# A planned attention kernel: fewer semaphore waits, phi(K) sums in column strips, and an order planned with queue times

## The chip, the cores and the metric

The kernel runs on one core of a Trainium2 chip. The metric is the device time of one execution in microseconds (us); lower is better. The engines are named as the profile names them: PE (matmul; PEld is its weight load), DVE (vector), ACT (scalar), POOL (GpSimd) and SP (here the queue that issues DMAs).

## What is computed

Two attention blocks over the same input `x` (2048 x 512, bf16), 32 heads of 16, mixed by a gate:

```python
g = sigmoid((x * gate_w).sum(-1))
# A: softmax attention
p = softmax(q @ k.T * 16 ** -0.5);  a = (p @ v) @ A_wo
# B: linear attention, phi(t) = where(t > 0, t + 1, exp(t)) + 1e-6
kv = phi(k).T @ v;  z = phi(k).sum(over the sequence)
b = ((phi(q) @ kv) / (phi(q) @ z + 1e-6)) @ B_wo
out = g * a + (1 - g) * b
```

## The kernel before

**A planner writes the order.** While the program is built, a Python planner keeps a clock for each engine, a cost for each step, and for each tile the time of its last write and reads. It emits again and again the step that can start first; a list of tasks with release and due times (the table `TS`, in rounds) and some settings (`DEF`) decide between steps. The five instruction streams that come out are fixed: each engine runs its own in order, and semaphores hold an instruction until what it needs is there. So a step that waits holds everything behind it on its engine.

**Block A** goes in 32 rounds (8 heads of one parity group, 512 queries). PE makes score tiles of 128 keys x 512 queries, up to four heads beside each other in the rows of the array (`ps<-Qz,KT`). A tile is exponentiated in one of two ways. ACT does two tiles with one Exp (line 722) into P. Or DVE makes 16-bit integers that, read as bf16, are a rough exponential (line 634 for two tiles, line 673 for one), and POOL adds two constants to them (line 699), so that three terms with weighted copies of V (Vs, line 931) make up the sum. So a tile of DVE's needs three PV matmuls, one of ACT's needs one. PV matmuls (`ps<-P,Vp`, `ps<-Z,Vp`, `ps<-Z,Vs`) stand four beside each other in the columns of the array, in one bank (bank 7) for a whole round. At a round's end DVE transposes that bank (L959); each second round it takes reciprocals (L969), multiplies (L971) and transposes into OAT (L974).

**Everything else is tasks** that share the remaining bank 4: projections K (L871), Q (L900) and V (L922); the gate (L936 to L952); phi(K) and phi(Q) (Exp into eb on ACT, L981; two passes on DVE, L982 and L983); M = x.T phi(K) (L1003); the sums of phi(K), `t_z` (L1015); KV (L1036); the denominators `t_den` (L1061 to L1065); block B's output `t_bout` (L1077), which a transposing DMA on SP puts into OBT, the former xnat; and at last 16 output blocks `t_final`, each with four matmul steps of the B part (`ps<-wB,xnat`), four of the A part (`ps<-wB,OAT`), a pass by gg (L1110 on ACT, L1112 on DVE) and a DMA.

**Q loads.** Each Q projection is written to QT (L900) and copied to Qz by eight DMAs on SP. **The gate** is written to DRAM by four DMAs and read back in another layout by one (`ge<-gdram`), then used by DVE (L949).

**Waits.** `deps_of` lists what an instruction depends on; `_Eng.add` turns that into semaphore waits and leaves out one that the same engine has already waited for. Where an instruction has more than one wait, the first in the list goes inside it, and the others become instructions of their own ahead of it, which only wait (EVENT_SEMAPHORE, shown at line 1331).

**Costs.** A step of column-strip matmuls (`pe4`) is planned as the columns at 2.4 per ns + 8 ns for each group of four, at least 110 ns; a DMA issued by the planner as 60 ns of SP. PV steps of less than four matmuls are held back up to `PWN` ns (900). Where the plan leaves PE idle, filler matmuls (`ps<-warm`) stand.

Of the kernel before, what the change touches and what calls it, by code (L numbers as in the profile page):

```python
# [34 lines left out]
class _Eng:  # L35
    def __init__(self, name, sem, pipe):
        self.name = name
        self.sem = sem
        self.pipe = pipe
        self.free = 0.0  # L40
        self.ops = []
        self.n = 0
        self.inc_idx = []
        self.inc_val = []
        self.semval = 0
        self.waited = {}
# [81 lines left out]
def bass_gated_mix__mha_block__linear_attn_block__prompt_kernel(  # L128
# [42 lines left out]
    with ExitStack() as es:  # L171
        _cnt = [0]

        def SB(shape, dt, name):
            _cnt[0] += 1
            return es.enter_context(nc.sbuf_tensor(f"{name}_{_cnt[0]}", list(shape), dt))
# [85 lines left out]
        r_outt = [R(f"outt{i}") for i in range(2)]  # L262
        r_ge, r_gg, r_gd = R("ge"), R("gg"), R("gd")

        def deps_of(E, reads, writes):
            deps = []
            for res in reads:
                if res.w is not None:
                    deps.append(res.w)
            for res in writes:  # L270
                if res.w is not None:
                    deps.append(res.w)
                deps.extend(res.r.values())
            if E is PE:
                deps = [d for d in deps if not (isinstance(d, _Ev) and d.E is PE)]
            return deps
# [598 lines left out]
        def t_q(n, fixed=None):  # L875
# [51 lines left out]
        def t_vs(t8, vb):  # L927
            yield ("WAIT", lambda: ("v", t8 // 2, 2 * vb) in flags and ("v", t8 // 2, 2 * vb + 1) in flags and (t8 < 2 or st["pv_round"] > t8_rounds[t8 - 2][-1]))
            sl = slice(32 * vb, 32 * vb + 32)
            for w in range(1, NTERM):  # L930
                yield dl(265, lambda w=w: nc.vector.tensor_scalar(Vs[:, t8 % 2, w - 1, sl, :], Vp[:, t8, sl, :], WTS[w], None, op0=ALU.mult),
                         [r_Vp[t8][2 * vb], r_Vp[t8][2 * vb + 1]], [r_Vs[t8 % 2][w - 1][vb]])
            yield ("FLAG", lambda: V_ready.add(("s", t8, vb)))

        def t_gate():
# [12 lines left out]
            yield ("DMA", ge[:], gdram.rearrange("(k p) -> p k", p=128), semGE, 16, 3000.0, [r_gd], [r_ge], "nc", True)  # L948
            yield dv(100, lambda: nc.vector.tensor_scalar(ge[:], ge[:], 1e30, None, op0=ALU.min), [r_ge], [r_ge])  # L949
            phi_free[0] = True  # L950
            yield dv(100, lambda: nc.vector.tensor_scalar(gg[:], ge[:], 1.0, None, op0=ALU.add), [r_ge], [r_gg])
# [3 lines left out]
        def aout(r):  # L955
# [9 lines left out]
            if par == 0:  # L965
# [8 lines left out]
            yield dl(636, lambda: nc.vector.transpose(OAT[:, t8, 512 * qc:512 * (qc + 1)], T2[:]), [r_T2], [r_OAT[t8][qc]])  # L974
# [2 lines left out]
        def phi(b, dst_ap, dst_res):  # L977
            yield ("WAIT", lambda: phi_free[0] or phi_free[1])
            i = 0 if phi_free[0] else 1
            phi_free[i] = False  # L980
            yield ac(476, lambda: nc.scalar.activation(eb[:, i, :], bank(b), ACT.Exp), [r_bank[b]], [r_eb[i]])  # L981
            yield dv(345, lambda: nc.vector.tensor_scalar(eb[:, i, :], eb[:, i, :], 1.0, 1e-6, op0=ALU.min, op1=ALU.add), [r_eb[i]], [r_eb[i]])  # L982
            yield dv(609, lambda: nc.vector.scalar_tensor_tensor(dst_ap, bank(b), 1.0 + 1e-6, eb[:, i, :], op0=ALU.add, op1=ALU.max),  # L983
                     [r_bank[b], r_eb[i]], dst_res)
            yield ("FREE", b)
            phi_free[i] = True
# [20 lines left out]
        def t_z():  # L1007
            yield ("WAIT", lambda: all(("phik", tb) in flags for tb in range(NKB)))
            b = yield ("BANK",)
            for i in range(NCC):  # L1010
                for h in range(2):
                    yield pe_step(8, 140, [mm(bank(b)[:, i:i + 1], phiK[:, tb, 128 * i:128 * (i + 1)], ones[:, 0:1], start=(tb == 0), stop=(tb == NKB - 1))
                                           for tb in range(8 * h, 8 * h + 8)], [*r_phiK[8 * h:8 * h + 8], r_ones], [r_bank[b]])
            for i in range(NCC):
                yield dv(200, lambda i=i: nc.vector.tensor_scalar(Zbd[:, i, :], zmask[:], bank(b)[:, i:i + 1], None, op0=ALU.mult),  # L1015
                         [r_bank[b], r_zmask], [r_Zb])
            yield ("FREE", b)
            yield ("FLAG", lambda: flags.add("z"))
# [32 lines left out]
        def t_den(qc):  # L1051
# [4 lines left out]
            for qbl in range(4):  # L1056
                for i in range(NCC):
# [216 lines left out]
        while True:  # L1274
# [113 lines left out]
```

## Time and profile before

| | |
|---|---|
| time, median of 3 runs | 684.74 us (684.66 to 685.08) |
| the profiled execution | 684.91 us, span 683.2 us |
| granted PE clock over the span, mean | 0.99 |
| instructions in the profile | 20908 |
| exponentials on ACT (L722) | 671 |
| passes on DVE for two tiles (L634), for one (L673) | 310, 86 |
| filler matmuls | 95 |

A row of the profile has the busy time of a group of instructions, the mean of one, and the idle time of its engine just before them with what ended it. "L722" is line 722 of the kernel. Matmuls overlap each other, and so do consecutive passes on ACT, DVE and POOL, so the mean duration of one is longer than the step from one start to the next. The clock column of a stretch is the share of full speed that PE was granted.

### The profile page before, as it was taken

To read this page: it belongs to the slowest core of one execution; us is meant where nothing else is said; L and a number is where in the kernel's file an instruction comes from. 1 tells how busy PE (TensorE), PEld (TensorE's weight loads), DVE (VectorE), ACT (ScalarE), POOL (GpSimd) and SP (SyncE) were. 2 spreads that over 40 slices of the span, in tenths; PEclk is the share of its full clock that TensorE was granted. 3 is DMA by queue.
4 is the path that set the end of the run, shared out by engine and by line. 5 is a ranking of instruction groups with operands and counts; after the bars stand their busy time and mean duration, and the time that the engine had idled before them with its cause. 6 is when DMAs were issued, how large, how long until landed. Compare 5 with 4: busy or idle time off the path is not lost.

```text
span 683.2 us, 20908 instructions
## 1 busy us (share of the span) xinstructions
PE 645.9 (95%) x8412; PEld 192.7 (28%) x8412; DVE 576.0 (84%) x691; ACT 645.7 (95%) x712; POOL 436.5 (64%) x736
## 2 busy tenths in 40 slices
PE   8999899999999999999999999999999999999995
PEld 3422222222323222223322223222222222222222
DVE  5788689898876777889999899889889888989892
ACT  6799799999999999999999999999999999999991
POOL 4465577566755567676655566667666677878781
PEclk9999999999999999999999999999999999999998
DMA  5700000001010000200000101101000200000000
GB/s 130 222 24 23 4 2 4 8 8 26 2 40 2 2 1 2 51 8 2 2 4 15 25 9 34 10 25 25 25 10 17 33 17 18 1 10 10 10 10 32
DMA packets 35208, 15.39 MB, mean 23 GB/s; under 512 B 26532, under 2 KB 35108, under 8 KB 35112
## 3 DMA queue, kind: packets, MB, share of 16 engines
q1 hardware_dynamic: 34056, 13.79, 8.5%
q8 instruction: 67, 1.10, 0.7%
q10 hardware_dynamic: 1056, 0.26, 0.2%
q14 instruction: 29, 0.24, 0.1%
HBM read 6.30 MB, written 2.11 MB: 12 GB/s over the span
## 4 chain that ended last, share of the span: by engine, by line
PE 60%; ACT 14%; DVE 11%; issue 9%; POOL 3%; DMA 2%; SPq 0%; POOLq 0%; ACTq 0%; DVEq 0%
PE ps L327 60%; ACT P L722 13%; DVE Z L634 6%; POOL Z L699 3%; DVE T L959 1%; DVE Z L673 1%; DVE OBn L1077 1%; DMA xnat<-OBn 1%; DMA xnat<-in_A_x_dram 1%; DMA ge<-gdram 0%; ACT eb L981 0%; DVE T L971 0%; SPq L311 0%; DVE Vp L922 0%; DVE outt L1112 0%
## 5 line engine op out<-in xcount | busy, mean ns | idle before, releaser
L722 ACT ACTIVATE P<-ps 128x1024 bf16<-128x1024 f32 x671 | 629.1, 1054 | 16.7 <-PE ps L327 15.0
L699 POOL INT64_ADD Z<-Z x718 | 431.4, 616 | 228.5 <-DVE Z L634 203.9
L634 DVE TENSOR_SCALAR Z<-ps 128x1024 int16<-128x1024 f32 x310 | 377.3, 1217 | 72.4 <-PE ps L327 59.3
L327 PE MATMUL ps<-Qz,KT 32*128 32x512 bf16 x2048 | 262.5, 385 | 18.7 <-DVE Z L634 8.3
L327 PE MATMUL ps<-P,Vp 128*17 128x512 bf16 x1342 | 232.8, 385 | 1.3 <-DVE T L959 0.6
L327 PE MATMUL ps<-Z,Vs 128*17 128x512 bf16 x1412 | 228.2, 383 | 1.1 <-DVE Z L634 0.7
L327 PE MATMUL ps<-Z,Vp 128*17 128x512 bf16 x706 | 160.2, 384 | 0.4 <-DVE T L959 0.4
L327 PEld LDWEIGHTS ps<-Qz,KT 32*128 32x128 bf16 x2048 | 68.9, 91 | 269.1 <-ACT P L722 233.9
L327 PEld LDWEIGHTS ps<-P,Vp 128*17 128x17 bf16 x1342 | 51.3, 88 | 67.7 <-issue 40.2
L327 PEld LDWEIGHTS ps<-Z,Vs 128*17 128x17 bf16 x1412 | 51.6, 88 | 54.0 <-issue 35.0
L673 DVE TENSOR_SCALAR Z<-ps 128x512 int16<-128x512 f32 x86 | 58.1, 676 | 0.3 <-PE ps L327 0.3
L327 PE MATMUL ps<-xT,wA 128*32 128x512 bf16 (+1 forms) x528 | 37.5, 382 | 4.1 <-DVE phiK L983 3.2
L327 PEld LDWEIGHTS ps<-Z,Vp 128*17 128x17 bf16 x706 | 35.3, 88 | 12.8 <-issue 6.8
L327 PE MATMUL ps<-warm 128*17 128x512 bf16 (+8 forms) x104 | 30.9, 356 | 1.4 <-POOL warm L381 1.4
L959 DVE STREAM_TRANSPOSE T<-ps 128x512 f32<-128x512 f32 x32 | 22.7, 709 | 7.4 <-PE ps L327 7.4
L327 PE MATMUL ps<-wB,OAT 128*32 128x512 bf16 x256 | 21.2, 393 | 2.7 <-DVE OAT L974 2.7
L983 DVE SCALAR_TENSOR_TENSOR phiK<-ps,eb 128x512 bf16<-128x512 f32 x32 | 21.9, 685 | 0.8
L327 PE MATMUL ps<-wA,xT 128*32 128x256 bf16 x512 | 20.8, 275 | 0.4 <-DVE Vp L922 0.3
L327 PE MATMUL ps<-phiK,xnat 128*32 128x512 bf16 x256 | 19.5, 382 | 0.4 <-DVE Zbd L1015 0.4
L981 ACT ACTIVATE eb<-ps 128x512 f32<-128x512 f32 x32 | 19.9, 620 | 0.0
L327 PE MATMUL ps<-xT,wB 128*32 128x512 bf16 x256 | 19.6, 383 | 0.2 <-DVE phiK L983 0.2
L327 PE MATMUL ps<-wB,xT 128*32 128x512 bf16 x256 | 19.3, 383 | 0.3 <-DVE phiK L983 0.2
(73 smaller groups left out, 238.0 us busy)
## 6 DMA issues: line engine op xcount, KB each, us to landing
out_dram<-outt SPq DMA_DIRECT2D x16, 128.0 KB, 1.7
Qz<-QT SPq DMA_DIRECT2D x120, 16.0 KB, 1.8
wB<-in_B_wqkv_dram SPq DMA_DIRECT2D x3, 512.0 KB, 6.6
xnat<-in_A_x_dram SPq DMA_DIRECT2D x3, 512.0 KB, 8.6
wA<-in_A_wqkv_dram SPq DMA_DIRECT2D x10, 128.0 KB, 3.0
xnat<-in_A_x_dram SPq DMA_DIRECT2D x4, 128.0 KB, 3.3
wB<-in_B_wo_dram SPq DMA_DIRECT2D x1, 512.0 KB, 4.3
wB<-in_A_wo_dram SPq DMA_DIRECT2D x1, 512.0 KB, 3.8
```

The lines of the kernel that those rows point to most:

```text
L327: return lambda: nc.tensor.matmul(o, lhsT=l, rhs=r, start=start, stop=stop, skip_group_check=True)
L634: res.append(C(DV, 400, 1135, lambda: nc.vector.tensor_scalar(Z[:, zs[0], :], bank(5, 2), ZB, 0.0, op0=ALU.add, op1=ALU.max), [r_bank[5], ...
L673: res.append(C(DV, prio, 606, lambda b=b, z=z, h=h: nc.vector.tensor_scalar(Z[:, z, 512 * h:512 * (h + 1)], bank(b), ZB, 0.0, op0=ALU.add, ...
L699: return C(PO, 300, 160 + 0.416 * (hi - lo), lambda: nc.gpsimd.int64_add(Z[:, zw, lo:hi].bitcast(I64), Z[:, z0, lo:hi].bitcast(I64), cst), ...
L722: return C(AC, 500, 434 * n + 42, lambda: nc.scalar.activation(P[:, slot, 0:512 * n], bank(2 * g, n), ACT.Exp, scale=ESC), [r_bank[2 * g + ...
L959: yield dv(637, lambda: nc.vector.transpose(T1[:, par, :], bank(7)), [r_bank[7]], [r_T1[par]])
L981: yield ac(476, lambda: nc.scalar.activation(eb[:, i, :], bank(b), ACT.Exp), [r_bank[b]], [r_eb[i]])
L983: yield dv(609, lambda: nc.vector.scalar_tensor_tensor(dst_ap, bank(b), 1.0 + 1e-6, eb[:, i, :], op0=ALU.add, op1=ALU.max), [r_bank[b], r_ ...
L1077: yield dv(609, lambda: nc.vector.tensor_tensor(OBn[:, o, :].rearrange("p (h d) -> p h d", d=16), bank(b).rearrange("p (h d) -> p h d", d= ...
```

## The change

Four things are changed together.

1. **Waits.** Each engine keeps with every semaphore increment a copy of what it had waited for by then (`snap`). Who waits for that increment takes over all that the copy holds, and later waits for those are left out. `deps_of` sorts the dependencies by the planned time, the latest first, so the latest goes inside the instruction.
2. **Sums of phi(K).** `ones` has 64 columns, not 2. Before, each of the 64 products used a full 128 x 128 phi(K) block against one column of ones; now each is four matmuls, one for 32 columns of the array, against 64 columns of ones. The result is read from column 64 i of the bank.
3. **Planned costs.** SP is charged 630 ns for a Qz load or the strided gate load, 1290 ns for a transposing DMA and 380 ns for others. `pe4` is charged 4 ns a group over its columns, at least 57 ns. Where DVE and POOL use the port that they share at the same time, the later is delayed (`_Port`, `port`). Some durations and DMA times are other numbers.
4. **The order.** Settings (`DEF`) and due times (`TS`) are others, and with the new costs the whole order comes out anew. In `TS`, `t_bout` for query chunk qc is released at round 15.9 + 6.2 qc, before at 16.2 + 1.11 qc, and due at 16.9 + 4.2 qc, before at 17.9 + 2.5 qc; so its last four steps (34.5) are released after the last of the 32 rounds' scores.

```diff
+            if isinstance(d, _Ev):
+                for k2, v2 in d.E.snap[val - 1].items():
+                    if self.waited.get(k2, 0) < v2:
+                        self.waited[k2] = v2
...
+            self.snap.append(dict(self.waited))
...
-    DEF = {"SKEW": 4, "DSL": 0.0, "DTOL": 500.0, "PWE": 0.0, "PWT": 0.0, "PWN": 900.0, "TPR": 650, "RIDE": 1200.0, "HP": 115.0, "HD": 115.0, "NDB": 2, "SLK": 50.0, "UEX": 0.2, "TOP": 800, "B4": 1, "ROOM": 4, "STP": 2}
+    DEF = {"SKEW": 4, "DSL": 80.0, "DTOL": 500.0, "PWE": 0.0, "PWT": 0.0, "PWN": 400.0, "TPR": 620, "RIDE": 1200.0, "HP": 115.0, "HD": 115.0, "NDB": 2, "SLK": 50.0, "UEX": 0.2, "TOP": 420, "B4": 1, "ROOM": 3, "STP": 2}
...
-        ones = SB([128, 2], BF16, "ones")
+        ones = SB([128, 64], BF16, "ones")
...
+                deps.extend((res.tr[e2], d) for e2, d in res.r.items())
+            deps.sort(key=lambda v: -v[0])
...
+            if E is DV and isinstance(dur, _Port):
+                if port["p0"] <= start < port["p1"]:
+                    dur = max(dur, port["p1"] - start + dur.tail)
+                port["d0"], port["d1"] = start, start + dur + E.pipe
+            elif E is PO:
+                if port["d0"] <= start < port["d1"]:
+                    dur = max(dur, port["d1"] + 470.0 - E.pipe - start)
+                port["p0"], port["p1"] = start, start + dur + E.pipe
...
-            return ("OP", PE, len(groups) * max(cols / 2.4 + 8, 110.0), fns, reads, writes, "col")
+            return ("OP", PE, len(groups) * max(cols / 2.4 + 4, 57.0), fns, reads, writes, "col")
...
-                    yield pe_step(8, 140, [mm(bank(b)[:, i:i + 1], phiK[:, tb, 128 * i:128 * (i + 1)], ones[:, 0:1], start=(tb == 0), stop=(tb == NKB - 1))
-                                           for tb in range(8 * h, 8 * h + 8)], [*r_phiK[8 * h:8 * h + 8], r_ones], [r_bank[b]])
+                    yield pe4(64, [mm4(bank(b)[:, 64 * i:64 * (i + 1)], phiK[:, tb, 128 * i:128 * (i + 1)], ones[:], tb == 0, tb == NKB - 1)
+                                   for tb in range(8 * h, 8 * h + 8)], [*r_phiK[8 * h:8 * h + 8], r_ones], [r_bank[b]])
...
+                iss = 1290.0 if tr is True else 630.0 if tr == "nc" or c.name[0] == "Q" else 380.0
```

Three places of the new order. The first is DVE where it comes to the gate (`ge`). The rows from QT on, before:

```order
L900 TENSOR_SCALAR QT<-ps 128x512
L971 TENSOR_TENSOR T_25<-T_23,rec 128x2x16x16
L634 TENSOR_SCALAR Z<-ps 128x1024
L974 STREAM_TRANSPOSE OAT<-T_25 128x512
L982 TENSOR_SCALAR eb<-eb 128x512
L634 TENSOR_SCALAR Z<-ps 128x1024
L949 TENSOR_SCALAR ge<-ge 128x16
L983 SCALAR_TENSOR_TENSOR phiK<-ps,eb 128x512
```

and in the changed kernel (its line numbers are 22 higher here):

```order
L922 TENSOR_SCALAR QT<-ps 128x512
L656 TENSOR_SCALAR Z<-ps 128x1024
L996 STREAM_TRANSPOSE OAT<-T_25 128x512
L695 TENSOR_SCALAR Z<-ps 128x512
L656 TENSOR_SCALAR Z<-ps 128x1024
L953 TENSOR_SCALAR Vs<-Vp 128x576
L656 TENSOR_SCALAR Z<-ps 128x1024
L1004 TENSOR_SCALAR eb<-eb 128x512
L971 TENSOR_SCALAR ge<-ge 128x16
L1005 SCALAR_TENSOR_TENSOR phiK<-ps,eb 128x512
```

`ge` moved back: five steps stood between QT and it, now seven. The second place is SP from the gate's way out to DRAM on, before (`waits` shows which semaphores; `s_gd` counts the gate's arrival in DRAM):

```order
L311 DMA gdram<-eb 1x512 [waits s_act]
L311 DMA gdram<-eb 1x512 x3
L311 DMA Qz<-QT 16x512 [waits s_dve]
L311 DMA Qz<-QT 16x512 x3
L311 DMA Qz<-QT 16x512 [waits s_pe]
L311 DMA Qz<-QT 16x512 x2
L310 DMA ge<-gdram 128x16x1 [waits s_gd]
L311 DMA Qz<-QT 16x512
```

and in the changed kernel:

```order
L333 DMA gdram<-eb 1x512 [waits s_act]
L333 DMA gdram<-eb 1x512 x3
L333 DMA Qz<-QT 16x512 [waits s_dve]
L333 DMA Qz<-QT 16x512 x2
L332 DMA ge<-gdram 128x16x1 [waits s_gd]
L333 DMA Qz<-QT 16x512 x5
```

The load of `ge` went ahead of four Qz loads, and the wait of the second half of the Qz loads for PE is left out. The third place is the end of PE's stream, from the last PV matmuls ahead of the output blocks on, before:

```order
L327 MATMUL ps<-wB,xnat 32x512 x16
L327 MATMUL ps<-wB,OAT 32x512 x12
L327 MATMUL ps<-P,Vp 17x512
L327 MATMUL ps<-Z,Vs 17x512 x4
L327 MATMUL ps<-P,Vp 17x512
L327 MATMUL ps<-Z,Vs 17x512
L327 MATMUL ps<-Z,Vp 17x512
L327 MATMUL ps<-P,Vp 17x512
L327 MATMUL ps<-Z,Vs 17x512 x2
L327 MATMUL ps<-P,Vp 17x512 x2
L327 MATMUL ps<-Z,Vs 17x512 x4
L327 MATMUL ps<-wB,OAT 32x512 x16
```

(the first two rows stand there four times in turn, these being the last), and in the changed kernel:

```order
L349 MATMUL ps<-KVbd,phiK 32x128 x16
L349 MATMUL ps<-Z,Vs 17x512 x4
L349 MATMUL ps<-warm 17x512
L349 MATMUL ps<-warm 17x192
L349 MATMUL ps<-Z,Vs 17x512 x2
L349 MATMUL ps<-KVbd,phiK 32x128 x16
L349 MATMUL ps<-wB,xnat 32x512 x16
L349 MATMUL ps<-wB,OAT 32x512 x12
L349 MATMUL ps<-wB,xnat 32x512 x16
L349 MATMUL ps<-wB,OAT 32x512 x20
```

The last PV matmuls went ahead of the four output blocks, and the last four steps of `t_bout` (`KVbd,phiK`), which were done long before, stand among them now.

More of the change, by code (lines that the diff above doesn't have):

```diff
@@ L46, in __init__ @@
         self.waited = {}
+        self.snap = []
         self.cands = []
@@ L85, in add, with __new__ @@
             self.inc_val.append(self.semval)
+            self.snap.append(dict(self.waited))
         self.ops.append((waits, fn, inc, dma_sem))
         return _Ev(self, idx)
+class _Port(float):
+    def __new__(cls, dur, tail):
+        p = float.__new__(cls, dur)
+        p.tail = tail
+        return p
 class _Res:
@@ L263, in bass_gated_mix__mha_block__linear_attn_block__prompt_kernel @@
         r_ge, r_gg, r_gd = R("ge"), R("gg"), R("gd")
+        port = {"p0": 0.0, "p1": 0.0, "d0": 0.0, "d1": 0.0}
         def deps_of(E, reads, writes):
@@ L268, in deps_of @@
                 if res.w is not None:
-                    deps.append(res.w)
+                    deps.append((res.tw, res.w))
             for res in writes:
                 if res.w is not None:
[L272 to L276, printed above, removed]
+                    deps.append((res.tw, res.w))
+                deps.extend((res.tr[e2], d) for e2, d in res.r.items())
+            deps.sort(key=lambda v: -v[0])
+            return [d for _, d in deps if not (E is PE and isinstance(d, _Ev) and d.E is PE)]
         def emit(E, dur, fns, reads=(), writes=(), name=""):
@@ L906, in t_q @@
                     p0 = 32 * j + 16 * par
-                    yield ("DMA", Qz[p0:p0 + 16, s, par, :], QT[p0:p0 + 16, a, :], semQ[s], tot, 2500.0, [r_QT[a]], [r_Qz[s][par]], False, j == 0)
+                    yield ("DMA", Qz[p0:p0 + 16, s, par, :], QT[p0:p0 + 16, a, :], semQ[s], tot, 2200.0, [r_QT[a]], [r_Qz[s][par]], False, j == 0)
             for par in range(2):
@@ L930, in t_vs @@
             for w in range(1, NTERM):
-                yield dl(265, lambda w=w: nc.vector.tensor_scalar(Vs[:, t8 % 2, w - 1, sl, :], Vp[:, t8, sl, :], WTS[w], None, op0=ALU.mult),
+                yield dl(_Port(216, 84), lambda w=w: nc.vector.tensor_scalar(Vs[:, t8 % 2, w - 1, sl, :], Vp[:, t8, sl, :], WTS[w], None, op0=ALU.mult),
                          [r_Vp[t8][2 * vb], r_Vp[t8][2 * vb + 1]], [r_Vs[t8 % 2][w - 1][vb]])
@@ L947, in t_gate @@
             r_gd.w = _Raw(semGD, 64)
-            yield ("DMA", ge[:], gdram.rearrange("(k p) -> p k", p=128), semGE, 16, 3000.0, [r_gd], [r_ge], "nc", True)
+            yield ("DMA", ge[:], gdram.rearrange("(k p) -> p k", p=128), semGE, 16, 3600.0, [r_gd], [r_ge], "nc", True)
             yield dv(100, lambda: nc.vector.tensor_scalar(ge[:], ge[:], 1e30, None, op0=ALU.min), [r_ge], [r_ge])
@@ L970, in aout @@
             t2 = T2[:].rearrange("p (q a d) -> p a q d", a=2, d=16)
-            yield dl(642, lambda: nc.vector.tensor_tensor(t2, t1[:, :, :, 0:16], rec[:].unsqueeze(3).to_broadcast([128, 2, 16, 16]), ALU.mult),
+            yield dl(_Port(593, 465), lambda: nc.vector.tensor_tensor(t2, t1[:, :, :, 0:16], rec[:].unsqueeze(3).to_broadcast([128, 2, 16, 16]), ALU.mult),
                      [*r_T1, r_rec], [r_T2])
@@ L981, in phi @@
             yield ac(476, lambda: nc.scalar.activation(eb[:, i, :], bank(b), ACT.Exp), [r_bank[b]], [r_eb[i]])
-            yield dv(345, lambda: nc.vector.tensor_scalar(eb[:, i, :], eb[:, i, :], 1.0, 1e-6, op0=ALU.min, op1=ALU.add), [r_eb[i]], [r_eb[i]])
+            yield dv(_Port(337, 199), lambda: nc.vector.tensor_scalar(eb[:, i, :], eb[:, i, :], 1.0, 1e-6, op0=ALU.min, op1=ALU.add), [r_eb[i]], [r_eb[i]])
             yield dv(609, lambda: nc.vector.scalar_tensor_tensor(dst_ap, bank(b), 1.0 + 1e-6, eb[:, i, :], op0=ALU.add, op1=ALU.max),
@@ L1011, in t_z @@
                 for h in range(2):
[L1012 to L1013 removed]
+                    yield pe4(64, [mm4(bank(b)[:, 64 * i:64 * (i + 1)], phiK[:, tb, 128 * i:128 * (i + 1)], ones[:], tb == 0, tb == NKB - 1)
+                                   for tb in range(8 * h, 8 * h + 8)], [*r_phiK[8 * h:8 * h + 8], r_ones], [r_bank[b]])
             for i in range(NCC):
[L1015 removed]
+                yield dv(200, lambda i=i: nc.vector.tensor_scalar(Zbd[:, i, :], zmask[:], bank(b)[:, 64 * i:64 * i + 1], None, op0=ALU.mult),
                          [r_bank[b], r_zmask], [r_Zb])
@@ L1064, in t_den @@
             dv_ap = dn[:, a, :].rearrange("p (q h) -> p q h", q=4)
-            yield dl(215, lambda: nc.vector.tensor_tensor(dv_ap, dv_ap, ge[:, 4 * qc:4 * qc + 4].unsqueeze(2).to_broadcast([128, 4, 32]), ALU.mult),
+            yield dl(_Port(196, 68), lambda: nc.vector.tensor_tensor(dv_ap, dv_ap, ge[:, 4 * qc:4 * qc + 4].unsqueeze(2).to_broadcast([128, 4, 32]), ALU.mult),
                      [r_dn[a], r_ge], [r_dn[a]])
@@ L1315, in bass_gated_mix__mha_block__linear_attn_block__prompt_kernel @@
                 _, o, i, sem, tot, lat, rd, wr, tr, chk = c.fns[1]
-                fin = dma(SP, o, i, sem, tot, lat, reads=rd, writes=c.writes, transpose=(tr is True), noncontig=(tr == "nc"), name=c.name)
+                iss = 1290.0 if tr is True else 630.0 if tr == "nc" or c.name[0] == "Q" else 380.0
+                fin = dma(SP, o, i, sem, tot, lat, reads=rd, writes=c.writes, transpose=(tr is True), noncontig=(tr == "nc"), name=c.name, issue=iss)
                 if not chk:
```

2 lines of the change are left out of this document (1 added, 1 removed).

## The prediction

> **What bounds the kernel now.** I read the page first: shares, chain, groups.
>
> ```profile
> PE 645.9 (95%) x8412; PEld 192.7 (28%) x8412; DVE 576.0 (84%) x691; ACT 645.7 (95%) x712; POOL 436.5 (64%) x736
> ...
> PE 60%; ACT 14%; DVE 11%; issue 9%; POOL 3%; DMA 2%; SPq 0%; POOLq 0%; ACTq 0%; DVEq 0%
> ...
> L722 ACT ACTIVATE P<-ps 128x1024 bf16<-128x1024 f32 x671 | 629.1, 1054 | 16.7 <-PE ps L327 15.0
> ...
> L634 DVE TENSOR_SCALAR Z<-ps 128x1024 int16<-128x1024 f32 x310 | 377.3, 1217 | 72.4 <-PE ps L327 59.3
> ...
> L673 DVE TENSOR_SCALAR Z<-ps 128x512 int16<-128x512 f32 x86 | 58.1, 676 | 0.3 <-PE ps L327 0.3
> ```
>
> PE and ACT are both at 95%. ACT has one job that nobody shares, 671 exponentials of two score tiles each. By stages, columns being length, then busy time of PE, PEld, DVE, ACT, POOL, then clock and DMA:
>
> ```profile
> 400.00:540.00 140.00, 131.88 (x1795) 40.27 (x1797) 125.70 (x146) 137.42 (x153) 93.45 (x156) 1.00 0.11 22
> 540.00:666.80 126.80, 122.57 (x1470) 32.95 (x1473) 111.44 (x124) 125.73 (x135) 96.63 (x164) 1.00 0.04 11
> 666.80:683.20 16.40, 8.48 (x137) 3.59 (x129) 3.97 (x6) 1.44 (x3) 1.13 (x2) 0.80 0.10 33
> ```
>
> Up to 666.8 ACT has hardly a gap, and PE is 94 to 97% covered. After that stands a tail of 16.4 us in which everything is idle by turns. The price of an exponential is its start-to-start time, since consecutive ones overlap (timeline of ACT):
>
> ```profile
> 118.96 0.62 ACT L981 ACTIVATE eb<-ps 128x512 f32<-128x512 f32 x1
> 119.44 3.81 ACT L722 ACTIVATE P<-ps 128x1024 bf16<-128x1024 f32 x4
> 123.08 0.66 ACT L981 ACTIVATE eb<-ps 128x512 f32<-128x512 f32 x1
> ```
>
> Four take 123.08 - 119.44 = 3.64 us, 0.91 each. So time can go in three ways: fewer exponentials, the few places where ACT stands, and the tail. The sum is made against the profiled execution, 684.9 us (span 683.2), 0.2 above the median 684.74.
>
> **The waits that are left out.** Instructions that only wait:
>
> ```profile
> L1331 ACTq EVENT_SEMAPHORE  x580: 17/17/38, 8.0 to 679.8; - x194
> L1331 PEldq EVENT_SEMAPHORE  x410: 51/51/374, 3.2 to 671.2; - x137
> L1331 POOLq EVENT_SEMAPHORE  x394: 17/17/43, 26.2 to 666.6; - x197
> L1331 DVEq EVENT_SEMAPHORE  x317: 21/21/50, 6.2 to 679.3; - x159
> ```
>
> The changed program keeps 3 of ACT's, 18 of DVE's, none of POOL's, and 407 of PE's. ACT's 577 x 17 ns would be 9.8 us if they stood in the stream. But 580 waits stand ahead of 712 instructions, and the run of four above still went at 0.91; they pass while the instruction before is at work. ACT: nothing taken. On PE the number stays; what changes is which wait is inside, and a stand-alone one that comes last delays its matmul by up to 51 ns.
>
> ```profile
> PE ps L327 <- DVE Z L634: 9.1, 32, 0.8
> ...
> PEld ps L327 <- DVE Z L634: 5.1, 17, 0.4
> ```
>
> 49 x 51 ns = 2.5 us at most, 0 at least: I take **-1.0**.
>
> **The gate's load.** SP, DVE, PE and ACT around 70 us, then the waits of 66 to 76 us, then a stretch with its clock:
>
> ```profile
> 63.91 4.32 SPq L311 DMA_DIRECT2D Qz<-QT  x7
> 68.27 0.59 SPq L310 DMA_DIRECT2D ge<-gdram  x1
> ```
> ```profile
> 71.54 0.17 DVE L949 TENSOR_SCALAR ge<-ge 128x16 f32<-128x16 f32 x1 [2.79 <-DMA ge<-gdram]
> ...
> 72.36 0.93 PE L327 MATMUL ps<-xT,wA 128*32 128x512 bf16 x8 [2.74 <-DVE phiK L983]
> ...
> 73.88 1.02 ACT L722 ACTIVATE P<-ps 128x1024 bf16<-128x1024 f32 x1 [3.41 <-PE ps L327]
> ```
> ```profile
> ACT P L722 <- PE ps L327: 3.9, 2, 3.4
> ```
> ```profile
> 72.00:76.00 4.00, 3.64 (x30) 0.59 (x30) 2.97 (x7) 1.61 (x2) 1.28 (x2) 0.57 0.00 0
> ```
>
> The planner charged 60 ns for a DMA issue; seven Qz issues took 4.32 us, 0.62 each, and `ge` stood behind them. DVE came to `ge` 2.79 us early, all DVE work queued behind it, PE stopped, ACT lost 3.9 us. In the new order three Qz issues stand between QT and `ge`, not seven: 1.9 us of queue, then 71.54 - 68.27 = 3.3 to landing, 5.2 after QT. DVE has after QT three full passes, a half, a transpose, a Vs and an eb pass ahead of `ge`:
>
> ```profile
> L982 DVE TENSOR_SCALAR eb<-eb 128x512 f32<-128x512 f32 x32 | 14.6, 455 | 3.3 <-ACT eb L981 3.3
> ...
> L974 DVE STREAM_TRANSPOSE OAT<-T 128x512 bf16<-128x512 bf16 x16 | 11.2, 700 | 0.1
> ```
>
> 3 x 1.217 + 0.676 + 0.700 + 0.455 = 5.5 us even without Vs and without a wait (each pass overlaps the next by under 0.1), so `ge` is there when DVE is. What is late next is nothing on this path: the phi pass behind `ge` has its operands. I take **-3.9**; ends 0 and -3.9.
>
> **The sums of phi(K).** PE, two windows, and ACT's waits of 205 to 224 us:
>
> ```profile
> 211.17 0.55 PE L327 MATMUL ps<-ones,phiK 128*128 128x1 bf16 x16
> ```
> ```profile
> 209.00:212.40 3.40, 3.11 (x52) 1.36 (x44) 2.81 (x4) 3.40 (x4) 2.16 (x4) 1.00 0.00 0
> 212.40:215.90 3.50, 3.44 (x30) 0.70 (x30) 1.50 (x3) 2.47 (x4) 1.88 (x4) 0.51 0.02 5
> ```
> ```profile
> ACT P L722 <- PE ps L327: 1.3, 2, 0.9
> ```
>
> After a stretch of one-column matmuls the clock was 0.51 for 3.5 us, and ACT lost 1.3. With 64 columns in four strips the array works longer, so I expect no drop: -1.3, ends 0 and -1.7 (half of 3.4). Against it stand 256 matmuls for 64. The nearest row is the block product, 16 matmuls in 0.41:
>
> ```profile
> 538.11 0.41 PE L327 MATMUL ps<-KVbd,phiK 128*32 128x128 bf16 x16 [0.64 <-DVE OBn L1077]
> ```
>
> A step of 32 lasts at most 0.8, against about 0.3 for 8 one-column ones (0.55 for 16): 8 steps, 0 to +4 us of PE; I take +1.2, half hidden. Together **-0.7**.
>
> The Trainium skill (TensorE: Matmul & The Clock Gate, What's actually happening) has the clock drop after an idle window of about 3.4 us. Of the two drops here the first is near to that (PE idle 2.74), the second is not (PE covered 3.11 of the 3.40 before it); by the rule alone the strips would change nothing there, and this term would be +0.6, the sum 677.3.
>
> **The new order.** Counted over the whole program: exponentials 671 to 667, half passes on DVE (line 673) 86 to 94, groups of PV matmuls 899 to 927 since a partial group now goes after 400 ns, not 900. Fewer exponentials: 4 x 0.91 = **-3.6** (ends -3.6 and 0, if PE sets the pace). The 8 halves cost DVE 8 x 0.676 = 5.4 us, covered by its idle 107; if that cover were gone, 5.4. A PV group is 0.22 (start to start):
>
> ```profile
> 672.20 0.38 PE L327 MATMUL ps<-Z,Vs 128*17 128x512 bf16 x1
> ...
> 672.42 0.38 PE L327 MATMUL ps<-Z,Vp 128*17 128x512 bf16 x1
> ```
>
> 28 x 0.22 = 6.2 us on an engine that is 95% covered; part replaces filler matmuls (95 to 87). Ends 0 and +6.2; near the PE rows' 94 to 97% I take a third, **+2.0**. Early on, the new order holds 6,400 filler columns ahead of the last K tile of the first group, not 3,968, at 0.22 us for 512 1.0 us more; **+0.8**, ends 0 and +1.6. Elsewhere ACT's waits for PE are small: of 15.0 in all, 3.9 and 1.3 are above, 5.6 lie ahead of 40 us:
>
> ```profile
> ACT P L722 <- PE ps L327: 5.6, 4, 3.2
> ```
>
> 4.2 are left. Planner's costs closer to the rows (0.63 for a Qz issue, 1.29 for a transposing one, delays of DVE at the port it shares with POOL) may save some: **-1.0**, ends 0 and -4.2.
>
> **The tail.**
>
> ```profile
> 666.16 1.04 PE L327 MATMUL ps<-wB,xnat 128*32 128x512 bf16 x16
> ...
> 673.71 0.72 DVE L959 STREAM_TRANSPOSE T<-ps 128x512 f32<-128x512 f32 x1 [7.18 <-PE ps L327]
> ...
> 679.86 0.69 ACT L1110 ACTIVATE outt<-ps,gg 128x512 bf16<-128x512 f32 x1 [2.04 <-DMA out_dram<-outt]
> ```
>
> Now four output blocks (6.0 us of PE) stand ahead of the last PV groups, and DVE waits 7.18. The new order puts the PV groups first: up to 6.0 us sooner. But the last four block-B products, released after the last scores, now come there too. Each needs an OBn pass, a transposing DMA, then its output block:
>
> ```profile
> 533.60 7.40 SPq L307 DMA_TRANSPOSE xnat<-OBn  x4
> ```
>
> ```profile
> xnat<-OBn SPq DMA_TRANSPOSE x16, 2.5
> ```
>
> Four in a row take SP 7.4 us, with two OBn buffers; the fourth is issued three quarters of that, 5.6 us, after the first, and lands 2.5 later. Taking the first at the end of the last PV group (estimate): 8.1, then the last output block 1.5 (a quarter of 6.0), then as now from outt on 683.2 - 679.86 = 3.3. That is 12.9, and starts about 1.3 after the last exponential (two shifts of 0.6 on POOL): 14.2 against 16.4. The clock may halve while PE waits, up to 1.5 more. I take **-1.5**; ends -5.6 (the transposes hidden: 1.3 + 683.2 - 673.7, or 10.8, for 16.4) and +1.
>
> **Sum.** 684.9 - 1.0 - 3.9 - 0.7 - 3.6 + 2.0 + 0.8 - 1.0 - 1.5 = 676.0.
>
> **Rivals.** A: the above, 676.0. For it: each stall has its row and its cause in the order. Chance 0.48.
> B: PE sets the pace; the 28 groups cost 6.2 and the small waits stay: 676.0 + 4.2 + 1.0 = 681.2. For it PE's 97%, against it PE's room in fillers. 0.18.
> C, slower: SP works in order, and the transposes, whose due times are now later, stand between the Qz loads of the last rounds and wait there for DVE's OBn. A Qz load that is so pushed back by 7.4 us and is needed at once stops PE and ACT for as long, with the clock halved after it (1.7): 9.1 a time, two such 676.0 + 18.2 = 694.2. It decides where QT is written less than 7.4 + 8 x 0.62 + 1.8 (Qz landing, page) = 14 us before its first scores. Against it: no wait on Qz is on the lists now. 0.12, with other new stalls.
>
> ```profile
> Qz<-QT SPq DMA_DIRECT2D x120, 16.0 KB, 1.8
> ```
>
> D: the clock drops near the sums all the same, from the waits of about 0.4 us around them and not from their narrow matmuls; the strips only cost 0.6: 676.0 + 1.3 = 677.3. 0.08. The rule of the Trainium skill's page on TensorE named above would have it so, in that only idle time counts.
> E: the change does not do what it says, DVE still waits for `ge`: 676.0 + 3.9 = 679.9. 0.08.
> F: all small waits go, and the tail gives its 5.6: 676.0 - 3.2 - 4.1 = 668.7. 0.06.
>
> **Numbers.** A measurement of this kernel tells 0.2% (1.4 us) from no change. Faster: A, D, E, F and two thirds of B, 0.82; within 0.2%: the rest of B, 0.06; slower: C, 0.12. The range 667 to 684 takes in F with a little to spare and the unknown ends above B; it leaves out C and some ends of the others, 2 in 10.
>
> **What would show it.** Right: 667 exponentials at 0.91; no DMA wait over 0.3 at `ge` and clock 1.0 there; clock 1.0 through the sums; the first transpose of the last accumulator within 2.5 us of the last exponential; stand-alone waits gone from ACT with its 0.91 unchanged. Wrong: ACT's waits for PE above 15.0 in all (B or C), a wait on Qz (C), a tail over 16.4.

## The result, and the profile after

The changed kernel takes 669.93 us (median of 4 runs, 668.75 to 670.68) against 684.91 (684.66 to 685.53) before on the same chip: a ratio of 0.9778, 95% interval 0.9761 to 0.9795, so 15.0 us less. The forecast was 676.0 with a range of 667 to 684: the sign and the range hold, the gain is 6 us larger than the sum said. The profiled execution is one of 670.68 us, its span 668.9.

The page of the changed kernel (its lines are 22 higher), in the order of the forecast: shares, chain, then the groups of exponentials and of DVE's full and half passes.

```profile
PE 642.4 (96%) x8612; PEld 192.4 (29%) x8612; DVE 577.1 (86%) x699; ACT 637.1 (95%) x708; POOL 443.8 (66%) x750
...
ACT 43%; PE 43%; DVE 10%; DMA 2%; POOL 1%; issue 1%; SPq 0%; ACTq 0%
...
L744 ACT ACTIVATE P<-ps 128x1024 bf16<-128x1024 f32 x667 | 620.7, 1072 | 9.5 <-PE ps L349 9.3
...
L656 DVE TENSOR_SCALAR Z<-ps 128x1024 int16<-128x1024 f32 x310 | 377.3, 1217 | 62.3 <-PE ps L349 59.2
...
L695 DVE TENSOR_SCALAR Z<-ps 128x512 int16<-128x512 f32 x94 | 63.5, 676 | 0.0
```

Two things have changed: ACT's waits for PE fell from 15.0 to 9.3 us, and in the chain that ended last "issue" fell from 9% to 1% and ACT rose from 14% to 43%, as much as PE. The chain alone proves little: a version below that gained nothing shows 2% of "issue" and 32% of ACT. By stages (length, busy PE, PEld, DVE, ACT, POOL, clock, DMA), these being the stretches that follow 400 us and then the tail:

```profile
400.00:540.00 140.00, 135.30 (x1709) 37.97 (x1706) 124.94 (x145) 139.31 (x155) 100.68 (x170) 1.00 0.05 14
540.00:651.50 111.50, 108.28 (x1382) 30.02 (x1378) 101.06 (x115) 111.50 (x122) 87.52 (x150) 1.00 0.06 15
651.50:668.90 17.40, 11.20 (x179) 5.14 (x175) 6.19 (x10) 1.40 (x3) 1.78 (x4) 0.90 0.32 62
```

ACT has hardly a gap left from 400 us on (139.3 of 140.0 and 111.5 of 111.5 us). The tail is the one stage that got longer, 17.4 us for 16.4.

**Where the 14.3 us of span went.** I went through ACT's starts one by one. From the first exponential to the last, each step from one start to the next was set against 0.903 us behind an exponential (the usual step there) and 0.476 behind an `eb` pass; what is over is called lost below. The stretches are by time in each kernel's own trace.

| | before | after | difference |
|---|---|---|---|
| exponentials x 0.903 | 671 | 667 | -3.6 |
| start of the first exponential | 10.15 | 10.53 | +0.4 |
| lost, 0 to 40 us | 6.1 | 7.0 | +0.9 |
| lost, 60 to 80 (`ge`) | 4.6 | 0.9 | -3.7 |
| lost, 200 to 230 (before: sums of phi(K)) | 2.5 | 1.1 | -1.4 |
| lost elsewhere | 21.8 | 13.8 | -8.0 |
| from the start of the last exponential to the end | 17.35 | 18.44 | +1.1 |

The unforeseen part is the second line from the bottom: 8 us that are spread over the whole kernel. The rows share out the whole span, so they add up to the 14.3 by the way they are made.

### The profile page after: what moved, and what is told of

It is laid out like the page before. It is cut to its first block, busy times and chain, and to the rows that moved or that the text cites. A ratio compares the mean times of both kernels' runs of the same rounds, so it can differ in the third digit from the quotient of the medians.

```text
span 668.9 us, 20031 instructions
## 1 busy us (share of the span) xinstructions
PE 642.4 (96%) x8612; PEld 192.4 (29%) x8612; DVE 577.1 (86%) x699; ACT 637.1 (95%) x708; POOL 443.8 (66%) x750
## 4 chain that ended last, share of the span: by engine, by line
ACT 43%; PE 43%; DVE 10%; DMA 2%; POOL 1%; issue 1%; SPq 0%; ACTq 0%
PE ps L349 43%; ACT P L744 42%; DVE Z L656 6%; POOL Z L721 1%; ACT eb L1003 1%; DVE T L981 1%; DMA xnat<-OBn 1%; DMA xnat<-in_A_x_dram 1%; DMA out_dram<-outt 1%; DVE Z L695 1%; DVE Vp L944 0%; DVE phiK L1005 0%; DVE KT L893 0%; DVE OBn L1099 0%; DVE eb L1004 0%
## 5 line engine op out<-in xcount | busy, mean ns | idle before, releaser
L744 ACT ACTIVATE P<-ps 128x1024 bf16<-128x1024 f32 x667 | 620.7, 1072 | 9.5 <-PE ps L349 9.3
L721 POOL INT64_ADD Z<-Z x732 | 438.6, 614 | 206.5 <-DVE Z L656 205.2
L349 PE MATMUL ps<-Z,Vs 128*17 128x512 bf16 x1428 | 246.2, 382 | 0.2 <-POOL Z L721 0.2
L349 PE MATMUL ps<-P,Vp 128*17 128x512 bf16 x1334 | 242.2, 382 | 1.5 <-DVE T L981 1.2
L349 PE MATMUL ps<-Z,Vp 128*17 128x512 bf16 x714 | 171.4, 382 | 0.8 <-DVE T L981 0.7
L349 PEld LDWEIGHTS ps<-Qz,KT 32*128 32x128 bf16 x2048 | 66.5, 91 | 262.9 <-ACT P L744 175.8
L349 PEld LDWEIGHTS ps<-Z,Vs 128*17 128x17 bf16 x1428 | 55.4, 88 | 54.9 <-issue 32.4
L695 DVE TENSOR_SCALAR Z<-ps 128x512 int16<-128x512 f32 x94 | 63.5, 676 | 0.0
L349 PEld LDWEIGHTS ps<-Z,Vp 128*17 128x17 bf16 x714 | 38.3, 88 | 14.4 <-issue 5.2
L349 PE MATMUL ps<-wB,xnat 128*32 128x512 bf16 x256 | 19.7, 402 | 2.2 <-DMA xnat<-OBn 2.2
```

The costliest lines, as they stand in the source:

```text
L349: return lambda: nc.tensor.matmul(o, lhsT=l, rhs=r, start=start, stop=stop, skip_group_check=True)
L695: res.append(C(DV, prio, 606, lambda b=b, z=z, h=h: nc.vector.tensor_scalar(Z[:, z, 512 * h:512 * (h + 1)], bank(b), ZB, 0.0, op0=ALU.add, ...
L721: return C(PO, 300, 160 + 0.416 * (hi - lo), lambda: nc.gpsimd.int64_add(Z[:, zw, lo:hi].bitcast(I64), Z[:, z0, lo:hi].bitcast(I64), cst), ...
L744: return C(AC, 500, 434 * n + 42, lambda: nc.scalar.activation(P[:, slot, 0:512 * n], bank(2 * g, n), ACT.Exp, scale=ESC), [r_bank[2 * g + ...
```

## The experiments

All ratios are against the kernel before on the same chip, in brackets their 95% interval. The kernel before has a median of 684.9 to 686.3 us on these chips; a gain in us is taken from the ratio, as its share of 684.9. Line numbers differ by a few between the versions. Theory O says that the new order brings the gain, theory W that stand-alone waits did more harm than the forecast allowed.

**The change to the waits alone.** The kernel before with `snap` and the sorted `deps_of` (point 1 of the change); the order stays.

> The kernel before in its old order, with only the waits changed (implied ones left out, the latest inside the instruction). Theory O (the new order brings the gain): 682.5 to 684.9 us, exponentials at 0.90 as before, and the waits of ACT for PE between 40 and 666 us, leaving out the two places at 70 and 214 us, stay as they are. Theory W (the stand-alone waits are what spread small delays over the whole kernel): about 677 us, most of the 8 us that the changed kernel gained outside its three named places.

681.62 us, 0.9915 (0.9888 to 0.9943): 5.8 us (3.9 to 7.7) from waits alone, in an order that is untouched. That is between O and W. The forecast had 1.0 and at most 2.5.

**The changed kernel with the waits of before.** The same edit backwards.

> The changed kernel in its new order, with the old way of making waits. Theory O: 670 to 672 us. Theory W: about 678 us, with delays of under 0.4 us between exponentials spread over the whole span.

675.0 us, 0.9829 (0.9806 to 0.9853), again between O and W. The changed kernel has 0.9778: half a per cent comes back, some 3.5 us here in the new order. So the waits are a quarter of the gain by this run, two fifths by the one above, and the rest is not theirs.

**One half of the change to the waits.** `snap` only; where two waits are left, the first in the list still goes inside.

```diff
+            if isinstance(d, _Ev):
+                for k2, v2 in d.E.snap[val - 1].items():
+                    if self.waited.get(k2, 0) < v2:
+                        self.waited[k2] = v2
...
+            self.snap.append(dict(self.waited))
...
                 deps.extend(res.r.values())
```

> The kernel before with one half of the change to the waits: those that are implied by others are left out, but where two remain the first in the list goes inside, as before, not the latest. Stand-alone waits fall as far as with both halves (ACT 5, POOL 4, DVE 29, PE 401), the order is that of before. Theory N (their number costs the time): 0.9915 within its interval, 0.989 to 0.994, as with both halves. Theory L (the latest wait being outside costs it): little of it, 0.996 to 0.999.

685.93 us, 0.9994 (0.9978 to 1.001). Some 1,290 of 1,740 stand-alone waits are gone, and nothing is gained: theory N has fallen. **The waits of ACT alone**, both halves:

```diff
+            if self.name == "act" and isinstance(d, _Ev):
...
+            if E is AC:
+                deps.sort(key=lambda v: -v[0])
```

> The kernel before with the change to the waits on ACT alone: ACT keeps 5 of 582 stand-alone waits, the other engines all of theirs (PE 412, POOL 398, DVE 319). Theory A (a wait ahead of an exponential delays that exponential, 577 x about 10 ns): most of the 5.8 us, 0.991 to 0.993. Theory E (ACT's waits pass while the exponential before is at work, and the time was lost where DVE, POOL and PE wait for each other and for ACT): 0.998 to 1.000.

684.6 us, 0.9992 (0.9975 to 1.0008): nothing either, theory E. What is left is which of two waits stands inside, above all on PE, which keeps some 400 stand-alone ones in all versions. The lists of waits (who waited for whom: us in total, times, longest) of the version with one half, then of the version with both:

```profile
PEld ps L333 <- ACT P L728: 235.4, 554, 1.2
...
PEld ps L333 <- issue: 153.8, 606, 0.8
```
```profile
PEld ps L332 <- ACT P L727: 177.1, 441, 1.3
PEld ps L332 <- issue: 127.9, 539, 0.8
PEld ps L332 <- DVE Z L639: 73.3, 176, 0.9
```

With the latest inside, 176 weight loads are seen to wait for DVE's passes, with one half 17 as before the change. These waits were there before, too, but the list booked them to ACT or to "issue". Timeline of the kernel before, a DVE pass and the score loads behind it, twice:

```profile
331.09 1.23 DVE L634 TENSOR_SCALAR Z<-ps 128x1024 int16<-128x1024 f32 x1
...
332.44 0.13 PEld L327 LDWEIGHTS ps<-Qz,KT 32*128 32x128 bf16 x4 [0.27 <-ACT P L722]
...
332.91 1.23 DVE L634 TENSOR_SCALAR Z<-ps 128x1024 int16<-128x1024 f32 x1
...
334.25 0.13 PEld L327 LDWEIGHTS ps<-Qz,KT 32*128 32x128 bf16 x4 [0.48 <-ACT P L722]
```

and of the kernel before with both halves:

```profile
400.89 1.23 DVE L639 TENSOR_SCALAR Z<-ps 128x1024 int16<-128x1024 f32 x1 [0.31 <-PE ps L332]
...
402.17 0.10 PEld L332 LDWEIGHTS ps<-Qz,KT 32*128 32x128 bf16 x4 [0.64 <-DVE Z L639]
```
```profile
412.66 1.21 DVE L639 TENSOR_SCALAR Z<-ps 128x1024 int16<-128x1024 f32 x1
...
413.92 0.10 PEld L332 LDWEIGHTS ps<-Qz,KT 32*128 32x128 bf16 x4 [0.38 <-DVE Z L639]
```

From DVE's end to the load are 0.12 and 0.11 us at first (331.09 + 1.23 = 332.32), then 0.05 and 0.05. Over the whole traces the two values are sharp. I took the score loads that follow column work with a stand-alone wait ahead of them, and of these the ones where DVE's end is the latest before the load. In the kernel before 129 of 224 begin 112 to 118 ns after it, and 2 begin after 50 to 56; with both halves 16 of 166, and 50. The two versions that gained nothing keep the late value, some 130 times each; the changed kernel has it 8 times. So a stand-alone wait that ends last costs about 62 ns, not its 51, and it ended last some 129 times, not 49. With 16 left, 113 x 62 = 7.0 us on PE went, and the time fell by 5.8. That this happens on PE is read from the traces; a kernel with the waits of PE alone changed was not run, nor one with those of DVE or POOL.

**The strips alone.** The kernel before, its order kept, each step of the sums made of strips.

```diff
-                    yield pe_step(8, 140, [mm(bank(b)[:, i:i + 1], phiK[:, tb, 128 * i:128 * (i + 1)], ones[:, 0:1], start=(tb == 0), stop=(tb == NKB - 1))
-                                           for tb in range(8 * h, 8 * h + 8)], [*r_phiK[8 * h:8 * h + 8], r_ones], [r_bank[b]])
+                    yield pe_step(8, 140, [f for tb in range(8 * h, 8 * h + 8)
+                                           for f in mm4(bank(b)[:, 64 * i:64 * (i + 1)], phiK[:, tb, 128 * i:128 * (i + 1)], ones[:], tb == 0, tb == NKB - 1)],
+                                  [*r_phiK[8 * h:8 * h + 8], r_ones], [r_bank[b]])
```

> The kernel before in its old order and with its old planned costs, only the sums of phi(K) made by 256 matmuls in column strips. If the one-column matmuls are what halves the clock at 212 us: no drop of the clock there, ACT's wait of 0.9 us at 215 gone, 683.4 to 684.4 us. If the drop comes from the waits around them: the drop stays, 684.9 to 686 us because the strips take longer on PE.

684.59 us, 0.9977 (0.9957 to 0.9996), some 1.6 us (0.3 to 2.9). The clock at the place, in the profile of this kernel:

```profile
209.00:212.40 3.40, 3.02 (x96) 1.15 (x92) 2.22 (x3) 3.40 (x5) 2.12 (x4) 1.00 0.00 0
212.40:215.90 3.50, 3.29 (x122) 1.61 (x120) 2.91 (x4) 3.50 (x5) 2.33 (x4) 1.00 0.02 5
```

No drop. But the one-column sums, too, dropped the clock only in some profiles: at 212.5 in the kernel before and at 213.4 in the version with `snap` alone, and not in the versions with both halves, with ACT's waits alone, or with `ge` early (below). ACT lost 0.9 to 1.1 us from 200 to 230 us in those three, and 1.2 here, against 2.5 in the two with a drop. And the changed kernel with the waits of before, which has the strips, drops its clock from 252.5 to 255.9, after its sums have ended at 249; PE was covered only 2.04 us of the 3.40 before that. So the gain fits a drop that comes less often, but that the strips keep it away is not shown, and the width of the matmuls is not all that decides.

**The load of `ge` alone.** The kernel before; on SP it goes ahead of the seven Qz issues.

```diff
+        k = next(i for i, v in enumerate(SP.ops) if v[3] is semGE)
+        SP.ops.insert(k - 7, SP.ops.pop(k))
```

> The kernel before, only the DMA that reads the gate back issued ahead of the seven Qz loads on SP, not behind them. If the queue on SP is the cause of the stall at 70 us: DVE no longer waits for it, no drop of the clock at 72 us, 680.3 to 681.3 us (3.9 us of ACT's waiting gone). If the wait only moves (Qz loads are 0.6 us later): 683 to 685 us.

680.61 us, 0.9915 (0.9889 to 0.9941), some 5.8 us (4.0 to 7.6). The loss at 60 to 80 us went from 4.6 to 0.4, and there is no half clock at 72.5 or at 212.5; another one came up, from 536.0 to 539.4, where the kernel before had none.

**All three together, and the parts of the order.** The kernel before with both halves of the waits, the strips and `ge` early; its order is otherwise kept.

> The kernel before, its order kept, with three local edits at once: the waits of the changed kernel, the sums of phi(K) as column strips, and the load of ge issued ahead of the seven Qz loads. Alone they gave 0.9915, 0.9977 and 0.9915. Theory S (each removes a stall of its own): the gains multiply, 0.9915 x 0.9977 x 0.9915 = 0.981, near 672, and the new order with its 4 exponentials fewer then adds only 0.3%. Theory V (part of the gain of each was the same halved clock at 212 us, which was gone in the profile of each of them): 0.983 to 0.986, and the new order adds 0.5 to 0.8%. In the profile, both expect no wait for ge at 70 us, and ACT's starts to lose 22 to 24 us beside its work in V, 20 to 22 in S, against 35.0 before and 22.9 in the changed kernel.

673.33 us, 0.982 (0.9802 to 0.9839), between S and V. Lost between the first exponential and the last: 22.6 us, as much as in the changed kernel (22.9). So the whole new order, beyond `ge`, is worth only the 4 exponentials, of which the tail takes a third back: spans 671.6 and 668.9, 2.7 us apart. Next, **the changed kernel with the settings and due times of before** (`DEF`, `TS`):

> The changed kernel with the settings and due times of before (DEF and TS), so with the new costs, waits and strips alone; 674 exponentials, 89 half passes, and the tail of before (four output blocks ahead of the last PV groups). Theory C (the planned costs make the order good, the settings matter little): 0.977 to 0.981 of before, as the changed kernel. Theory T (the settings and due times do it): 7 exponentials more than the changed kernel cost 6.3 us, the waits and strips stay, so 0.985 to 0.990.

680.33 us, 0.9927 (0.9908 to 0.9945), and **the changed kernel with the planned costs of before**, which has this in `emit` and at the issue of DMAs, and the old numbers elsewhere:

```diff
-            elif E is PO:
+            elif False:
...
-                iss = 1290.0 if tr is True else 630.0 if tr == "nc" or c.name[0] == "Q" else 380.0
+                iss = 60.0
```

> The changed kernel with its settings and due times, but the planned costs of before (60 ns for each DMA issue, 8 ns and at least 110 ns for each group of column strips, no delay at the shared port, the old DMA times); 668 exponentials, 88 half passes, the tail of the changed kernel. Theory C: the stall at ge comes back, since seven Qz issues are again charged 60 ns each, and small waits with it: 0.984 to 0.988. Theory T: within 0.2% of the changed kernel, 0.977 to 0.980, and no wait over 0.5 us for ge.

680.62 us, 0.9928 (0.9909 to 0.9948). Neither theory's time holds for either: each half of the new plan, with the new waits and strips, is 7 us slower than the old order with these and `ge` early. With the old costs the stall at `ge` is back, as theory C had it, and 4.6 of the 7 us are lost there. SP's queue and DVE:

```profile
63.69 4.33 SPq L333 DMA_DIRECT2D Qz<-QT  x7
68.06 0.59 SPq L332 DMA_DIRECT2D ge<-gdram  x1
```
```profile
71.25 0.17 DVE L971 TENSOR_SCALAR ge<-ge 128x16 f32<-128x16 f32 x1 [3.31 <-DMA ge<-gdram]
```

So the planned costs are what moves `ge`: with the new costs and the old settings only 0.4 us are lost from 60 to 80 us. That it is the cost of an issue among them is argued, since they were put back together. With the old settings there are 673 exponentials, and ACT has a new stall where PE does the steps of `t_kv` (L1025) ahead of the scores:

```profile
255.36 1.94 ACT L744 ACTIVATE P<-ps 128x1024 bf16<-128x1024 f32 x2 [3.12 <-PE ps L349]
```

**The tail.** The changed kernel, the last four `t_bout` released earlier:

```diff
-                add_task(t_bout(4 * qc + qbl), a[0] + a[1] * qc + a[2] * qbl, a[3] + a[4] * qc + a[5] * qbl, f"BO{qc},{qbl}")
+                add_task(t_bout(4 * qc + qbl), min(a[0] + a[1] * qc, 28.5) + a[2] * qbl, a[3] + a[4] * qc + a[5] * qbl, f"BO{qc},{qbl}")
```

> The changed kernel with the last four block-B products (t_bout of query chunk 3) released from round 28.5 on, not 34.5, so that their transposing DMAs are over before the last scores; the order is the same as in the changed kernel up to the last 260 of its 3148 rows on PE. 668.5 exponentials for 667, +1.4 us. Theory X (the transposes set the changed kernel's tail of 18.4 us): the tail falls to 12 to 15 us, the whole is 2 to 5 us less than the changed kernel, 0.970 to 0.975. Theory Y (the products only change places: PE has no room in the last rounds, and DVE's output passes there push out exponentials): within 0.2% of the changed kernel, 0.976 to 0.980.

670.32 us, 0.9777 (0.9758 to 0.9796), span 668.9: no change, the time of theory Y. The tail is 1.2 us shorter, and the last exponential starts 1.2 us later. The transposes are gone, and the wait of before is back in their place, DVE for four output blocks, then PE for DVE's chain:

```profile
659.85 0.72 DVE L981 STREAM_TRANSPOSE T<-ps 128x512 f32<-128x512 f32 x1 [7.34 <-PE ps L349]
...
662.48 1.05 PE L349 MATMUL ps<-wB,OAT 128*32 128x512 bf16 x16 [2.68 <-DVE OAT L996]
```

So I took both away, with PV matmuls ahead of output blocks once the last scores are planned:

```diff
-                    prio = X("TPR") if room else 500
+                    prio = 200 if st["s_done"] else X("TPR") if room else 500
```

> As e10_after_bout, but after the last scores the planner prefers PV matmuls to the output blocks, so the blocks fill PE while POOL's last shifts and then DVE's chain (transpose, reciprocal, product, transpose, 2.6 us) run; in e10 that chain began after all four blocks and PE waited 2.7 us for it. Theory X: the last OAT is ready 3 to 4 us sooner, span 665 to 666, 0.972 to 0.974. Theory Y (the changes of matmul shape between PV and blocks and the halved clock eat it): 0.976 to 0.978.

667.35 us, 0.9733 (0.9718 to 0.9747); the span 665.8 is as X said. The same pass of DVE comes 5.1 us sooner, and the last two output passes now wait for the two output buffers:

```profile
654.71 0.72 DVE L981 STREAM_TRANSPOSE T<-ps 128x512 f32<-128x512 f32 x1 [2.54 <-PE ps L349]
...
662.35 0.75 DVE L1134 TENSOR_SCALAR outt<-ps,gg 128x512 bf16<-128x512 f32 x1 [3.64 <-DMA out_dram<-outt]
662.65 0.69 ACT L1132 ACTIVATE outt<-ps,gg 128x512 bf16<-128x512 f32 x1 [3.80 <-DMA out_dram<-outt]
```

With four places for them, slots of P (the wait for the old places goes too; one line of the edit):

```diff
+            ob, rb = (P[:, qbl, 0:512], r_P[qbl]) if tail else (outt[:, o, :], r_outt[o])
```

> As e11_after_pv_first, but the last four output blocks are written from four places (slots of P, which is done with), not two, so that no pass waits for a DMA; in e10 these waits were 1.8 us on DVE and 2.1 on ACT. Theory X: 1.7 us less than e11, 0.969 to 0.972. Theory Y (the last pass then waits for PE instead): within 0.5 us of e11.

665.65 us, 0.971 (0.9695 to 0.9725), 1.7 less as X said: the fastest version, some 0.7% ahead of the changed kernel. Now the last pass waits for PE:

```profile
660.80 0.69 ACT L1133 ACTIVATE P<-ps,gg 128x512 bf16<-128x512 f32 x1 [2.33 <-PE ps L349]
```

## Why the prediction was right, and which terms were mis-sized

**Right: the way the time is made up.** ACT sets the pace, and time went through fewer exponentials and fewer stalls. 667 exponentials at 0.90 each gave the 3.6. Rivals B and C fell: ACT's waits for PE are 9.3 in all, not above 15.0, and there is no wait on Qz. So did D and E. The 669.9 is nearer to F's 668.7 than to my 676.0, but F is not what happened either: the small waits went, and the tail, which F had 5.6 us shorter, got longer. That the range held is in part luck, since the terms below miss in both directions.

**Right: `ge`, -3.9.** The load leaves SP 3 us earlier, DVE comes to it without a wait, and the clock stays. Alone it gave 0.9915, at least 4.0 us; the table has 3.7. SP and DVE, then the waits of ACT from 66 to 76 us, then a window with its clock, before and after:

```profile
65.22 0.59 SPq L332 DMA_DIRECT2D ge<-gdram  x1
...
69.28 0.58 DVE L971 TENSOR_SCALAR ge<-ge 128x16 f32<-128x16 f32 x1
```
```profile
ACT P L744 <- PE ps L349: 0.3, 1, 0.3
```
```profile
66.00:80.00 14.00, 11.06 (x118) 2.55 (x110) 8.85 (x16) 9.95 (x13) 5.40 (x9) 0.88 0.11 9
```
```profile
66.00:80.00 14.00, 13.78 (x169) 3.57 (x165) 11.75 (x17) 13.70 (x17) 7.93 (x14) 1.00 0.10 8
```

**Right in size, its reason open: the sums, -0.7 against -1.4 in the table and -1.6 alone.** The clock holds through them; they lie between 236 and 247 us now:

```profile
234.00:250.00 16.00, 14.00 (x375) 5.32 (x369) 12.42 (x15) 15.76 (x18) 9.60 (x18) 1.00 0.08 19
```

The 0.6 that I charged for longer work did not show in ACT's losses. The Trainium skill (TensorE: Matmul & The Clock Gate, What's actually happening) puts the drop down to an idle window of about 3.4 us. The trace does not agree: the drop at 212.5 us came after 3.40 us in which PE was covered 3.11, and the one at 72.5 after PE had been idle for 2.74. Rival D's waits of 0.4 us make no such window either. The profiles without a drop at the same place show that something else takes part; what it is stays open.

**Mis-sized: the waits, -1.0 against -5.8 in the old order and some -3.5 in the new.** This term failed. I put a price on the 49 waits that the list booked to DVE, at 51 ns each. But where a stand-alone wait ends last, the list names another engine or "issue", so it can't be used to count how often that is. The traces put some 129 in place of 49 and 62 ns in place of 51. What I said of ACT (577 waits, nothing) holds: 0.9992. The stand-alone waits that the changed kernel keeps on PE and on ACT:

```profile
L1354 PEldq EVENT_SEMAPHORE  x407: 51/51/932, 3.2 to 651.6; - x136
...
L1354 ACTq EVENT_SEMAPHORE  x3: 17/17/3791, 71.5 to 662.2; - x3
```

**Near in size, by luck: the small waits, -1.0 against -1.9.** Of the 8.0 us that are lost elsewhere no more, the old order with the three local edits also sheds 6.1, and 5.2 go with the change to the waits alone. So 1.9 remain for the new plan. I gave the planner's closer costs as the reason, and that is not shown: the two versions with half of the new plan lose over 2 us more there than the old order with the three edits.

**Mis-sized: the PV groups, +2.0 against about 0.** There are 28 more, as counted, but ACT lost no more than with the old order (22.9 and 22.6). The early K tile (+0.8) fits: +0.9 up to 40 us; that the fillers are the cause was not tested.

**Wrong in sign: the tail, -1.5 against +1.0.** At 17.4 us it is over the 16.4 that I had named as a sign of being wrong. The first transpose of the last accumulator did come soon, 653.76 or 2.2 us after the last exponential's end at 651.53. In the terms of the sum, the first transposing DMA was issued 0.5 us after that end (1.3 forecast) and the fourth landed 8.5 us later (8.1). What failed is the rest, 8.4 us in place of 4.8. Two output blocks were still to be done when the fourth landed, not one, because PE had waited for the landing of the first and then ran at half clock from 656.4 to 659.8 (0.90 over the tail). And the wait for the second output buffer, which I had left out of the sum, stands last. DVE's chain, too, was cut in two by a wait for an OBn buffer:

```profile
652.03 7.28 SPq L329 DMA_TRANSPOSE xnat<-OBn  x4
...
653.76 0.72 DVE L981 STREAM_TRANSPOSE T<-ps 128x512 f32<-128x512 f32 x1 [1.16 <-PE ps L349]
...
656.09 0.69 DVE L1099 TENSOR_TENSOR OBn<-ps,dn 128x512 bf16<-128x512 f32 x1 [1.22 <-DMA xnat<-OBn]
656.11 1.65 PE L349 MATMUL ps<-wB,xnat 128*32 128x512 bf16 x16 [2.17 <-DMA xnat<-OBn]
...
666.04 0.69 ACT L1132 ACTIVATE outt<-ps,gg 128x512 bf16<-128x512 f32 x1 [3.87 <-DMA out_dram<-outt]
```

With the rows of the table in place of the terms the sum is 684.9 - 8.0 (waits and small waits) - 3.7 - 1.4 - 3.6 + 0 + 0.9 + 0.4 (first exponential later) + 1.1 = 670.6, against 670.7 for the profiled execution. This is bookkeeping and no proof of the causes; those rest on the experiments.

## What to carry to other kernels

Where an instruction needs two waits, put the one that comes last inside it: together with leaving out some 1,290 early waits that was worth 0.8% here in an unchanged order, and leaving them out alone was worth nothing; and don't count late waits by the list of releasers, count how many starts follow the other engine's end by the same short time. A new plan should be measured against the old plan with the known stalls mended by hand: here three local edits gave some 12 of the 15 us, and the plans with only half of the change, costs or settings, ended 7 us behind the old one so mended. What is moved out of one place in the tail has to be followed to the last DMA, since each wait that went (output blocks ahead of PV, transposes, output buffers) uncovered the next.

## What was not expected of the hardware

- From the end of a DVE pass to the load that waits for it: 53 ns with the wait inside the instruction, 115 with it in an instruction of its own ahead, although that one is shown with 51.
- Outside the tail the halved clock lasted 3.4 us each time but one: after the same stall at `ge` it lasted from 72.3 to 82.6 us, three times as long, in the profile of the version with strips alone. It comes and goes at places whose order is the same (212 us), and came at 536 us in a kernel that only differed at 65 us.
- The landing of a DMA can matter more than its issue. The row of four transposing DMAs, 7.28 us in the tail and 7.40 before, is not four times 1.8: it holds SP's waits for OBn as well, and one alone takes SP 1.2 us, as this line of the kernel before shows (shortest, median and longest in ns). In the tail the first two landed 4.0 and 3.6 us after their issue, the other two after 2.5, and it was the first landing that DVE and PE waited for.

```profile
L307 SPq DMA_TRANSPOSE xnat<-OBn x16: 1188/1198/1998, 375.4 to 539.8; - x16
```
